# A fused linear-attention and two-MLP kernel on one Trainium2 core: all six moves of a step's output issued by SyncE, with an earlier range column, other stores and a bank of its own

## The chip, the cores and the metric

The kernel runs on one core of a Trainium2 chip (trn2). The metric is the device time of one execution in microseconds (us), as the median over several executions. The core has five engines: TensorE (PE, matmuls; its weight loads are listed as PEld), VectorE (DVE), ScalarE (ACT), GpSimd (POOL) and SyncE (SP, which here only issues DMA transfers). Each engine runs its own instructions in order; they meet through semaphores.

## The reference

Three parts follow one another. The first is a linear attention with a state per batch and head (4 batches, 8 heads, 768 steps, head size 40); the other two are MLPs over 3072 tokens.

```python
# attention, for t in range(S); state is D x D per batch and head
y[:, :, t] = einsum('bhd,bhde->bhe', r_t, state)
Sa    = einsum('bhde,bhe->bhd', state, a_t)
state = state * w_t[:, :, None, :] - einsum('bhd,bhe->bhde', Sa, b_t)
state = state + einsum('bhd,bhe->bhde', v_t, k_t)
# first MLP: d_model 320, d_ff 2048
h = x @ w_in;  x = (h * sigmoid(1.702 * h)) @ w_out
# second MLP: d_ff 1536
g = x @ w_gate;  out = (g * sigmoid(g) * (x @ w_val)) @ w_out2
```

The weights of the MLPs arrive as 64-bit floats and are turned into pairs of 32-bit values (a high and a low part) on the chip; each MLP product is computed from high and low parts (eight matmuls for a product with 320 inputs).

## The kernel before

The attention is cut into 12 steps of 64 time steps. Within a step everything is small matmuls on PE, copies on ACT and masked products on DVE; the state couples one step to the next. Two attention steps make the input of one step of the first MLP (512 tokens), so the first MLP has 6 steps (numbered 0 to 5) of 16 features each (a feature is 128 columns of d_ff). The second MLP also has 6 steps of 512 tokens, with 12 features each.

**The planner.** The attention and the first MLP are not written in a fixed order. Each piece of work is a task with an engine, an estimated cost, what it reads and writes, and a due time (class `Plan`). `order()` simulates the engines with these costs and returns all tasks sorted by their planned begin; where PE would have a gap it adds filler matmuls (`Up.warm`, line 453). Attention tasks have due times by step; those of the MLP are taken when nothing more urgent is ready. The conversion of the first MLP's weights is in this plan too.

**Moves of a step's output.** At the end of an attention step DVE writes the output into `su` (line 1194). `give` (line 1242) then moves it with six DMAs (line 1255) into the tile `xm`, with features on the partitions: three for the first half (`xm0`, issued by SP), three for the second (`xm1`, issued by ACT). ACT and DVE turn `xm` into the high and low parts of the MLP's input `xst` (lines 1262 to 1268).

**First MLP.** `h_part` computes one feature: eight matmuls into the PSUM tile `h` (line 495), Silu on ACT (503), a high part on ACT (509) and a low part `gl` on DVE (510). `o_part`, two features later, adds the product with `w_out` to three PSUM banks, `sums` (lines 522 to 529): `acc[0]` and `acc[1]` with 128 outputs each, and `acc[2]`, whose halves are two partial sums of the last 64 outputs. The weights of two features come from DRAM into one of two buffers `wo` by four DMAs on SP (line 485). After the 16th feature the sums are read out into `sg` buffers: `acc[0]` by DVE (548), `acc[1]` by ACT (545), the upper half of `acc[2]` by ACT (555), and DVE adds the lower half (557). Each result is stored to `x2s` in DRAM by a DMA that ACT issues (551, 559).

**The tail.** When the last attention task has begun (`layer_one`), the rest of the first MLP's tasks, the tail, is run by a loop in `build` (lines 1736 to 1749). After each task marked `last` (the `gl` of a feature) it takes 11 jobs of the conversion of the second MLP's weights (`down.prepare(11)`): loads into `cva` on SP (301), operations on ACT, DVE and POOL, and copies `wg` to `wg` on SP (1387). When 14 PE tasks are left it issues the loads of the second MLP's first input (`load_x(0)`), at 10 it starts to split it, and at 2 it starts the second MLP.

**Second MLP and flag.** `Down.run` does per feature an `h_part` (two groups of eight matmuls, line 1456) and, two features behind, an `o_part` (1475 to 1477). Behind feature 8 of the last step it calls `bad_flag` (line 1295): DVE reduces a column over the smallest weights seen (1299 to 1301), PE transposes it (1303), DVE reduces the row and writes the flag `bad`, by which a branch at the end chooses a slow general version.

Of the kernel before, what the change touches and what calls it, by code (L numbers as in the profile page):

```python
# [386 lines left out]
class Up:  # L387
# [9 lines left out]
    def __init__(self, tc, ctx, keep, cst, w_out, x2s, side):  # L397
# [12 lines left out]
        self.ph = [q.tile([128, 512], F32, name="h")]  # L410
        self.still = k.tile([128, 1], F32R, name="still")
        self.nc.vector.memset(self.still.bitcast(F32), 0.0)  # L412
        self.sums = q.tile([128, 3, 512], F32, name="sums")
        self.acc = [self.sums[:, i] for i in range(3)]
        self.tail = False
        self.hs, self.nsg = 0, 0

    def engine(self, e):
# [38 lines left out]
    def tasks(self, plan):  # L457
# [55 lines left out]
        def o_part(m, i):  # L513
# [24 lines left out]
            if not sp:  # L538
                return
            xs = self.x2s[:, n * m:n * m + n]  # L540
            for k in range(2):
                s = sg_slot()
                t = self.sg[s]
                if k:
                    add("ACT", 0.6, lambda t=t: nc.scalar.activation(out=t, in_=acc[1], func=ACTF.Copy, scale=1 / 1.702),
                        ("acc",), (f"sg{s}",))
                else:
                    add("DVE", 0.7, lambda t=t: nc.vector.tensor_scalar(
                        out=t, in0=acc[0], scalar1=1 / 1.702, scalar2=None, op0=ALU.mult), ("acc",), (f"sg{s}",),
                        port=False)  # L550
                add("ACT", 0.4, lambda t=t, k=k: nc.scalar.dma_start(out=xs[128 * k:128 * k + 128], in_=t),
                    (f"sg{s}",), (), kb=256)
            s = sg_slot()
            t = self.sg[s][0:64]
            add("ACT", 0.6, lambda: nc.scalar.activation(out=t, in_=acc[2][64:128], func=ACTF.Copy, scale=1 / 1.702),
                ("acc",), (f"sg{s}",))
            add("DVE", 0.72, lambda: nc.vector.scalar_tensor_tensor(  # L557
                out=t, in0=acc[2][0:64], scalar=1 / 1.702, in1=t, op0=ALU.mult, op1=ALU.add), ("acc",), (f"sg{s}",), port=False)
            add("ACT", 0.5, lambda: nc.scalar.dma_start(out=xs[256:320], in_=t), (f"sg{s}",), (), kb=128)

        lag = []
        for m in range(B * S // n):
# [10 lines left out]
class Attention:  # L573
# [668 lines left out]
    def give(self, plan, n, due):  # L1242
# [8 lines left out]
            moves.append((t[40 * s:40 * s + 40, 2:4], x[64:104, 2 + s:3 + s].to_broadcast([40, 2, 256]), "xm1"))  # L1251
        moves.append((t[80:120, 2:4], x[64:104, 2:4], "xm1"))
        for i, (o, s, k) in enumerate(moves):
            e, q, cost = ("ACT", nc.scalar, 0.76) if k == "xm1" else ("SP", nc.sync, 0.5)
            plan.add(e, cost, lambda o=o, s=s, q=q: q.dma_start(out=o, in_=s), ("su",), (f"{k}.{i}",), due, kb=80)
        m, half = divmod(n, 2)
        key = f"x{m % 2}.{half}"
# [36 lines left out]

def bad_flag(nc, tc, down, cst, least, good, bad):

    with tc.tile_pool(name="fl2", bufs=1, side="right") as p:
        m = p.tile([128, 1], F32, name="fl_f")
        nc.vector.tensor_reduce(out=m, in_=least, axis=AXL.X, op=ALU.min)
        nc.vector.tensor_scalar(out=m, in0=m, scalar1=TINY, scalar2=None, op0=ALU.is_ge)  # L1300
        nc.vector.tensor_tensor(m, m, good[:, 0:1], op=ALU.mult)
        ps = down.ph.tile([128, 512], F32, tag="gv", name="gv")[0:1, 0:128]
        nc.tensor.transpose(ps, m, cst[:, C_ID:C_ID + 128])
        q = p.tile([1, 1], F32, name="fl_q")
        nc.vector.tensor_reduce(out=q, in_=ps, axis=AXL.X, op=ALU.min)
        nc.vector.tensor_scalar(out=bad, in0=q, scalar1=0.5, scalar2=None, op0=ALU.is_lt)
# [29 lines left out]
class Down:  # L1336
# [168 lines left out]
    def run(self, last):  # L1505
        for m in range(NSTEP):
            parts = iter(())
            for f in range(NF2):
                if m + 1 < NSTEP:
                    if f == 5:  # L1510
                        self.load_x(m + 1)
                    elif f == 8:
                        parts = self.split_x(m + 1)
                if m + f:
                    self.prepare(f=f)
                    self.h_part(m, f)
                    self.lag.append((m, f))
                next(parts, None)
                if m:
                    self.look()  # L1520
                if m == NSTEP - 1 and f == 8:
                    last()
                self.prepare(8)
                if len(self.lag) > self.LAG:
                    self.o_part(*self.lag.pop(0))
                self.prepare(8)
        for x in self.lag:
            self.o_part(*x)
# [171 lines left out]
def build(  # L1700
# [4 lines left out]
    with ExitStack() as ctx:  # L1705
# [5 lines left out]
        with tc.block(schedule_with_timeline_sim=True):  # L1711
# [8 lines left out]
            with conv_ctx, down_ctx, tc.manual_schedule():  # L1720
                conv = Convert(tc, conv_ctx)
                with up_ctx:
# [9 lines left out]
                    first += [words(out1)[q, i] for q in range(4) for i in range(5)]  # L1732
                    down = Down(tc, down_ctx, cst, conv, weights, first, x2s, out, up, least)
                    left = sum(t.eng == "PE" for t in tail)
                    parts = iter(())
                    for t in tail:
                        if t.eng == "PE":
                            if left == 2:
                                down.begin()
                            left -= 1  # L1740
                        t.run()
                        if hasattr(t, "last"):
                            down.prepare(11)
                        if t.eng == "PE":
                            if left == 14:
                                down.load_x(0)
                            elif left == 10:
                                parts = down.split_x(0)
                            next(parts, None)
                down.work(down_ctx)  # L1750
                down.run(lambda: bad_flag(nc, tc, down, cst, least, good, bad))
            rv = nc.values_load(bad, min_val=0, max_val=1)
        with tc.If(rv > 0):
            general(
# [87 lines left out]
```

## Time and profile before

| what | value |
|---|---|
| median of 3 runs | 1118.22 us (1114.80 to 1118.37) |
| the profiled execution's own time | 1112.34 us |
| its span, first to last instruction | 1110.5 us |
| mean granted TensorE clock | 0.985 of full speed |
| PE busy | 1073.1 us (97%), 16682 matmuls |
| DVE / ACT / POOL busy | 702.2 / 436.0 / 98.2 us |

The profile is of one execution. A line number is that of the kernel before. "out<-in" names the tiles written and read. In the timeline a bracket at the end of a row gives the idle time of the engine just before the instruction and what ended it. ACTq and SPq rows are instructions of the queue of that engine that issue DMAs; their time is that of the issue, not of the transfer. Waits are inferred from semaphores, and a wait for several is put down to the last one.

### The profile page before, as it was taken

To read this page: it belongs to the slowest core of one execution; us is meant where nothing else is said; L and a number is where in the kernel's file an instruction comes from. 1 tells how busy PE (TensorE), PEld (TensorE's weight loads), DVE (VectorE), ACT (ScalarE), POOL (GpSimd) and SP (SyncE) were. 2 spreads that over 40 slices of the span, in tenths; PEclk is the share of its full clock that TensorE was granted. 3 is DMA by queue.
4 is the path that set the end of the run, shared out by engine and by line. 5 is a ranking of instruction groups with operands and counts; after the bars stand their busy time and mean duration, and the time that the engine had idled before them with its cause. 6 is when DMAs were issued, how large, how long until landed. Compare 5 with 4: busy or idle time off the path is not lost.

```text
span 1110.5 us, 38519 instructions
## 1 busy us (share of the span) xinstructions
PE 1073.1 (97%) x16682; PEld 892.6 (80%) x16682; DVE 702.2 (63%) x1406; ACT 436.0 (39%) x814; POOL 98.2 (9%) x115
## 2 busy tenths in 40 slices
PE   8999999899999999999999999999999999999987
PEld 7777777678778787888788878888888888888876
DVE  8976797989697887979653667643443343443221
ACT  3443646454343534344343656432222222222221
POOL 0131123320100000000000323210000000000000
PEclk9896999999999999999999999999999999999999
DMA  6265547664353543544224677430423434341000
GB/s 209 73 184 171 180 150 219 180 195 140 113 166 111 161 133 103 162 127 137 87 62 131 201 212 228 142 90 1 141 69 115 124 116 126 96 147 59 24 1 27
DMA packets 141011, 141.88 MB, mean 128 GB/s; under 512 B 16032, under 2 KB 131744, under 8 KB 140832
## 3 DMA queue, kind: packets, MB, share of 16 engines
q1 hardware_dynamic: 134784, 131.48, 39.1%
q10 hardware_dynamic: 6048, 7.86, 2.1%
q8 instruction: 132, 2.16, 0.8%
q14 instruction: 47, 0.39, 0.1%
HBM read 118.04 MB, written 13.11 MB: 118 GB/s over the span
## 4 chain that ended last, share of the span: by engine, by line
PE 87%; DVE 5%; issue 3%; DMA 2%; ACT 1%; SPq 1%; ACTq 0%; POOL 0%; DVEq 0%
PE gv L1456 24%; PE h L495 15%; PE sums L527 4%; PE oacc L1477 4%; PE oacc L1476 4%; PE oacc L1475 4%; PE sums L528 3%; PE sums L529 3%; PE h L453 3%; PE ps L1175 2%; PE sums L523 2%; PE ps L1098 2%; PE sums L522 2%; PE ps L1227 2%; PE ps L740 1%
## 5 line engine op out<-in xcount | busy, mean ns | idle before, releaser
L1456 PE MATMUL gv<-xst,wg 128*128 128x512 f32 x1152 | 279.9, 395 | 0.0
L1456 PEld LDWEIGHTS gv<-xst,wg 128*128 128x128 f32 x1152 | 213.4, 188 | 45.7
L495 PE MATMUL h<-xst,wi 120*128 120x512 f32 x768 | 197.1, 398 | 0.0
L1461 DVE TENSOR_TENSOR sg<-gv,sg 128x512 f32<-128x512 f32 x72 | 49.8, 692 | 186.5 <-PE gv L1456 184.4
L495 PEld LDWEIGHTS h<-xst,wi 120*128 120x128 f32 x768 | 140.5, 188 | 30.6
L503 ACT ACTIVATE sg<-h 128x512 f32<-128x512 f32 x96 | 57.2, 596 | 152.6 <-PE h L495 145.0
L1462 ACT ACTIVATE gh<-sg 128x512 fp32r<-128x512 f32 x72 | 45.5, 632 | 143.0 <-DVE sg L1461 143.0
L510 DVE TENSOR_TENSOR gl<-sg,gh 128x512 fp32r<-128x512 f32 x90 | 63.4, 704 | 60.2 <-ACT gh L509 60.0
L1460 ACT ACTIVATE sg<-gv 128x512 f32<-128x512 f32 x72 | 43.0, 597 | 136.6 <-PE gv L1456 136.6
L323 POOL TENSOR_TENSOR cvw<-cvu,cva 128x256 uint32<-128x256 uint32 (+2 forms) x89 | 71.6, 805 | 274.1 <-DVE cvu L315 168.5
L1476 PE MATMUL oacc<-wo,gh 128*128 128x320 f32 x288 | 89.0, 309 | 0.0
L1477 PE MATMUL oacc<-wo,gl 128*128 128x320 f32 x288 | 89.0, 309 | 0.0
L1475 PE MATMUL oacc<-wo,gh 128*128 128x320 f32 x288 | 89.0, 309 | 0.0
L527 PE MATMUL sums<-gh,wo 128*128 128x512 f32 x192 | 80.8, 421 | 2.9 <-DVE sg L557 2.6
L1463 DVE TENSOR_TENSOR gl<-sg,gh 128x512 fp32r<-128x512 f32 x72 | 49.9, 692 | 50.2 <-ACT gh L1462 50.2
L528 PE MATMUL sums<-gh,wo 128*128 128x512 f32 x192 | 75.5, 393 | 0.0
L529 PE MATMUL sums<-gl,wo 128*128 128x512 f32 x192 | 75.2, 392 | 0.0
L509 ACT ACTIVATE gh<-sg 128x512 fp32r<-128x512 f32 x96 | 60.7, 632 | 3.6 <-ACT sg L503 0.3
L788 DVE TENSOR_TENSOR tsol<-tsol,tmp 128x126 f32<-128x126 f32 (+22 forms) x217 | 56.3, 260 | 6.7
L780 DVE TENSOR_TENSOR tmp<-tsol,nsol 128x126 f32<-128x126 f32 (+22 forms) x217 | 55.8, 257 | 6.9
L453 PE MATMUL h<-still 128*128 128x512 f32 x183 | 58.3, 466 | 1.1 <-DVE still L412 1.1
L1476 PEld LDWEIGHTS oacc<-wo,gh 128*128 128x128 f32 x288 | 54.1, 188 | 3.2
(182 smaller groups left out, 1618.8 us busy)
## 6 DMA issues: line engine op xcount, KB each, us to landing
wo<-w_out SPq DMA_DIRECT2D x192, 160.0 KB
cva<-out SPq DMA_DIRECT2D x128, 128.0 KB
cva<-gv SPq DMA_DIRECT2D x96, 128.0 KB
kb<-kba SPq DMA_DIRECT2D x92, 104.0 KB
cva<-in_ab SPq DMA_DIRECT2D x64, 120.0 KB
r<-rT SPq DMA_DIRECT2D x48, 104.0 KB
vt<-vT SPq DMA_DIRECT2D x48, 104.0 KB
a<-kba SPq DMA_DIRECT2D x46, 104.0 KB
```

Of the source, the lines that this page charges most:

```text
L323: nc.gpsimd.tensor_tensor(w.bitcast(U32), u, lo, op=ALU.add)
L453: self.nc.tensor.matmul(self.ph[0], c.to_broadcast([128, 128]), c.to_broadcast([128, 512]), start=True, stop=True)
L495: nc.tensor.matmul(ps[:, 0:n], self.wi[:, b, 128 * f:128 * f + 128], x[:, a], start=(e == 0), stop=(e == 7))
L509: add("ACT", 0.63, lambda: nc.scalar.activation(out=hi, in_=sg, func=ACTF.Copy), (f"sg{s}",), (f"gh{d}",))
L510: add(("DVE", "POOL"), (0.74, 1.35), lambda e: self.engine(e).tensor_tensor(lo, sg, hi.bitcast(F32), op=ALU.subtract), (f"sg{s}", f"gh{d}" ...
L527: nc.tensor.matmul(acc[k], w[:, c:c + 128], hi, start=st, stop=False)
L528: nc.tensor.matmul(acc[k], w[:, 256 + c:384 + c], hi, start=False, stop=False)
L529: nc.tensor.matmul(acc[k], w[:, c:c + 128], lo, start=False, stop=sp)
L1456: nc.tensor.matmul(ps, w[:, b], x[:, a], start=(i == 0), stop=(i == 7))
L1475: nc.tensor.matmul(acc[k], hi[:, c], self.wo[:, f, 0], start=st, stop=False)
L1476: nc.tensor.matmul(acc[k], hi[:, c], self.wo[:, f, 1], start=False, stop=False)
L1477: nc.tensor.matmul(acc[k], lo[:, c], self.wo[:, f, 0], start=False, stop=sp)
```

## The change

- `give`: all six moves are issued by SP, with a planned cost of 0.6 each (before 0.5 on SP and 0.76 on ACT).
- Readout of the sums: ACT reads `acc[0]` and `acc[1]`, DVE both halves of `acc[2]`; the three stores are issued after all of these; `acc[2]` becomes a tile of its own (`third`) in place of the third bank of `sums`. In the tail SP issues the stores.
- Tail: the SP tasks (loads of `wo`) are put off until behind the next task marked `last`, and behind that task's conversion jobs; no conversion jobs are taken between two such tasks if a task of the readout lies between them; `load_x(0)` comes at 20 PE tasks left in place of 14.
- `bad_flag` becomes a generator: its column (DVE) is made behind feature 7 of the last step, the transpose and the rest behind feature 10.

```diff
@@ Up.__init__
-        self.sums = q.tile([128, 3, 512], F32, name="sums")
-        self.acc = [self.sums[:, i] for i in range(3)]
-        self.tail = False
+        self.sums = q.tile([128, 2, 512], F32, name="sums")
+        self.acc = [self.sums[:, 0], self.sums[:, 1], q.tile([128, 512], F32, name="third")]
+        self.tail, self.stores = False, tc.nc.scalar
@@ Up.tasks, o_part
+            first = len(plan.tasks)
+            moves = []
             for k in range(2):
                 s = sg_slot()
                 t = self.sg[s]
-                if k:
-                    add("ACT", 0.6, lambda t=t: nc.scalar.activation(out=t, in_=acc[1], func=ACTF.Copy, scale=1 / 1.702),
-                        ("acc",), (f"sg{s}",))
-                else:
-                    add("DVE", 0.7, lambda t=t: nc.vector.tensor_scalar(
-                        out=t, in0=acc[0], scalar1=1 / 1.702, scalar2=None, op0=ALU.mult), ("acc",), (f"sg{s}",),
-                        port=False)
-                add("ACT", 0.4, lambda t=t, k=k: nc.scalar.dma_start(out=xs[128 * k:128 * k + 128], in_=t),
-                    (f"sg{s}",), (), kb=256)
+                add("ACT", 0.6, lambda t=t, k=k: nc.scalar.activation(out=t, in_=acc[k], func=ACTF.Copy, scale=1 / 1.702),
+                    ("acc",), (f"sg{s}",))
+                moves.append((xs[128 * k:128 * k + 128], t, s, 256))
             s = sg_slot()
             t = self.sg[s][0:64]
-            add("ACT", 0.6, lambda: nc.scalar.activation(out=t, in_=acc[2][64:128], func=ACTF.Copy, scale=1 / 1.702),
-                ("acc",), (f"sg{s}",))
+            add("DVE", 0.65, lambda: nc.vector.tensor_scalar(
+                out=t, in0=acc[2][64:128], scalar1=1 / 1.702, scalar2=None, op0=ALU.mult), ("acc",), (f"sg{s}",),
+                port=False)
             add("DVE", 0.72, lambda: nc.vector.scalar_tensor_tensor(
                 out=t, in0=acc[2][0:64], scalar=1 / 1.702, in1=t, op0=ALU.mult, op1=ALU.add), ("acc",), (f"sg{s}",), port=False)
-            add("ACT", 0.5, lambda: nc.scalar.dma_start(out=xs[256:320], in_=t), (f"sg{s}",), (), kb=128)
+            moves.append((xs[256:320], t, s, 128))
+            for o, t, s, kb in moves:
+                add("ACT", 0.4, lambda o=o, t=t: self.stores.dma_start(out=o, in_=t), (f"sg{s}",), (), kb=kb)
+            for t0 in plan.tasks[first:]:
+                t0.out = True
@@ Attention.give
-            e, q, cost = ("ACT", nc.scalar, 0.76) if k == "xm1" else ("SP", nc.sync, 0.5)
+            e, q, cost = "SP", nc.sync, 0.6
@@ bad_flag
         nc.vector.tensor_tensor(m, m, good[:, 0:1], op=ALU.mult)
+        yield
         ps = down.ph.tile([128, 512], F32, tag="gv", name="gv")[0:1, 0:128]
@@ Down.run
-                if m == NSTEP - 1 and f == 8:
-                    last()
+                if m == NSTEP - 1 and f in (7, 10):
+                    next(last, None)
@@ build
-                    parts = iter(())
-                    for t in tail:
+                    parts, later, up.stores = iter(()), [], nc.sync
+                    for i, t in enumerate(tail):
+                        if t.eng == "SP":
+                            later.append(t)
+                            continue
...
                         if hasattr(t, "last"):
-                            down.prepare(11)
+                            ends = [hasattr(x, "last") for x in tail[i + 1:]] + [True]
+                            if not any(hasattr(x, "out") for x in tail[i + 1:i + 1 + ends.index(True)]):
+                                down.prepare(11)
+                            for x in later:
+                                x.run()
+                            later = []
                         if t.eng == "PE":
-                            if left == 14:
+                            if left == 20:
                                 down.load_x(0)
...
+                    for x in later:
+                        x.run()
                 down.work(down_ctx)
-                down.run(lambda: bad_flag(nc, tc, down, cst, least, good, bad))
+                down.run(bad_flag(nc, tc, down, cst, least, good, bad))
```

## Rows read from the trace of the kernel before

**Rows 1.** Stages: stretch, its length, busy time of each engine (instructions), clock, DMA.
```profile
70.00:125.00 55.00, 49.20 (x1479) 38.78 (x1481) 41.63 (x71) 24.73 (x53) 8.72 (x12) 0.81 0.55 169
...
642.00:654.00 12.00, 9.44 (x42) 7.39 (x41) 7.96 (x17) 7.88 (x17) 2.30 (x3) 1.00 0.72 217
...
718.00:1078.00 360.00, 360.00 (x1838) 312.40 (x1837) 142.64 (x268) 97.14 (x171) 4.48 (x6) 1.00 0.28 86
```

**Rows 2.** Waits of PE: what waited, for what; total us, times, longest.
```profile
PE gv L1303 <- DVE fl_f L1301: 2.9, 1, 2.9
PE sums L527 <- DVE sg L557: 2.6, 1, 2.6
...
PE ps L1012 <- ACT md L647: 1.7, 1, 1.7
PE ps L995 <- ACT tok L647: 1.6, 2, 1.1
```

**Rows 3.** Timeline around the flag: start us, us, engine, line, operation.
```profile
1074.95 3.89 PE L1456 MATMUL gv<-xst,wg 128*128 128x512 f32 x16
...
1080.33 0.69 DVE L1463 TENSOR_TENSOR gl<-sg,gh 128x512 fp32r<-128x512 f32 x1 [0.70 <-ACT gh L1462]
...
1083.58 3.89 PE L1456 MATMUL gv<-xst,wg 128*128 128x512 f32 x16
...
1089.07 3.89 PE L1456 MATMUL gv<-xst,wg 128*128 128x512 f32 x16
```

**Rows 4.** Timeline of ACT where step 4's sums are read out.
```profile
648.60 0.44 ACT L307 ACTIVATE cva<-cva 128x256 uint32<-128x256 uint32 x1 [1.29 <-DMA cva<-gv]
...
649.25 0.58 ACT L545 ACTIVATE sg<-sums 128x512 f32<-128x512 f32 x1
```

**Rows 5.** Timeline of ACT where step 5's sums are read out.
```profile
709.29 0.60 ACT L545 ACTIVATE sg<-sums 128x512 f32<-128x512 f32 x1 [2.21 <-PE sums L522]
...
710.65 0.59 ACT L555 ACTIVATE sg<-sums 64x512 f32<-64x512 f32 x1 [0.76 <-DVE sg L548]
```

**Rows 6.** Timeline of DVE in the same stretch.
```profile
709.92 0.69 DVE L548 TENSOR_SCALAR sg<-sums 128x512 f32<-128x512 f32 x1 [2.12 <-ACT sg L545]
711.27 0.68 DVE L557 SCALAR_TENSOR_TENSOR sg<-sums,sg 64x512 f32<-64x512 f32 x1 [0.66 <-ACT sg L555]
```

**Rows 7.** Tile xm: its moves, ns min/median/max; who waited (us, times).
```profile
L1255 ACTq DMA_DIRECT2D xm<-su x36: 772/809/1383, 66.9 to 595.9; - x36
L1255 SPq DMA_DIRECT2D xm<-su x36: 706/716/1422, 67.9 to 595.1; - x36
...
  ACT md L647: 9.4, 2
  ACT tok L647: 5.2, 2
```

**Rows 8.** Timeline of ACT at the fourth step's moves.
```profile
220.32 0.70 ACT L647 ACTIVATE md<-ps 104x640 f32<-104x640 f32 x1 [5.64 <-DMA xm<-su]
```

**Rows 9.** Timeline of SP (its DMA issues) at the second step's moves.
```profile
112.03 2.33 SPq L1255 DMA_DIRECT2D xm<-su  x3
```

**Rows 10.** Timeline of ACT in the same stretch.
```profile
118.42 1.32 ACT L1262 ACTIVATE xst<-xm 120x256 fp32r<-120x256 f32 x4
```

**Rows 11.** Timeline of PE in the same stretch.
```profile
125.51 2.11 PE L495 MATMUL h<-xst,wi 120*128 120x512 f32 x8
```

**Rows 12.** Filler matmuls of line 453 alone: stretch, length, busy time.
```profile
70.00:125.00 55.00, 18.30 (x48) 10.63 (x46) 0.81 0.55 169
```

**Rows 13.** SP's DMA issues in the first layer's tail.
```profile
635.85 1.80 SPq L485 DMA_DIRECT2D wo<-w_out  x4
...
640.29 2.73 SPq L1387 DMA_DIRECT2D wg<-wg  x4
643.11 1.98 SPq L485 DMA_DIRECT2D wo<-w_out  x4
```

**Rows 14.** The chain that ended last, in time: start us, us, what.
```profile
645.62 2.89 DMA cva<-gv
```

More of the change, by code (lines that the diff above doesn't have):

```diff
@@ L1295, in bad_flag @@
 def bad_flag(nc, tc, down, cst, least, good, bad):
+    assert not down.looks and not down.seen
     with tc.tile_pool(name="fl2", bufs=1, side="right") as p:
```

## Prediction, made before the result was known

> **What bounds the kernel now.** I read the table of stages first [rows 1]. From 718 to 1078 us TensorE (PE) is busy for all 360 us, so nothing that other engines gain there moves the end: time can only come from places where PE stands still, or where it runs work that is not needed. The reader should look for three of them. In 70 to 125 us PE is busy 49.20 of 55 us, but 18.30 us of this are filler matmuls of line 453 [rows 12], and the granted clock is 0.81 of the full 2.4 GHz, a mixture of both levels. There the end is set by the chain through DVE, ACT, DMA and PE of the attention steps, until the first group of the MLP starts at 125.51 us [rows 11]. In 642 to 654 us PE is busy 9.44 of 12 us. The third place needs the list of PE's waits [rows 2]: the flag's transpose waits 2.9 us for VectorE.
>
> Then I read the timeline around each of these, and the tile xm, which is what the six moves write [rows 7]. They cost 0.716 us each on SP and 0.809 us each on ACT, 36 on either, three and three in each of 12 steps. ACT is an in-order engine: the copies behind the three moves wait until su is ready and the moves are issued (9.4 us before md, 5.2 us before tok) [rows 7]. In the fourth step ACT stood still for 5.64 us before md [rows 8]. PE then waited 1.7 us for md, and in two other steps 1.6 us for tok [rows 2].
>
> **The change, part by part.**
>
> *The flag in two parts (line 1295).* From one feature's first matmuls to the next it takes 1083.58 - 1074.95 = 8.63 us across the flag and 1089.07 - 1083.58 = 5.49 us in the next one [rows 3]: 3.1 us lost. The three VectorE operations on the flag's column stand in program order behind the gl of feature 8, which starts only at 1080.33 [rows 3], after PE had finished that feature's matmuls, and the transpose stands in PE's queue in front of the next group. With the column reduced at feature 7 and the transpose issued at feature 10, its input is some 2 x 5.49 = 11 us old. What is left is the transpose itself. Bounds 2.8 to 3.1; I take 3.0. The result is there 11 us later, but feature 11 (5.49 us) and three more groups of output matmuls still follow, so nothing at the end waits for it.
>
> *Reading out the sums.* After the last group of step 5, ACT and VectorE had nothing else to do, and still the four reads ran one behind the other: ACT 709.29, DVE 709.92, ACT 710.65, DVE 711.27 [rows 5, 6], 2.66 us in all; they wait for one another although they read three banks, since all three banks are one tile. With the third bank a tile of its own, ACT reads banks 0 and 1 (2 x 0.60 = 1.2 us) beside VectorE's two operations on the third (0.68 + 0.69 = 1.4 us). At the end of step 4, ACT came to its first read only at 649.25, behind conversion work that itself waited 1.29 us for a load [rows 4], and PE's next group waited 2.6 us for the last read, the only such wait of the run [rows 2]. The change also leaves out the 11 conversion jobs ahead of such a readout. 1.4 us fit under the one group of h matmuls (7.26 us for four groups, below, so 1.8) that PE runs in between. Bounds: 0, if something else holds ACT or VectorE, to 2.6; I take 2.5. At the other five ends PE doesn't wait, so they give nothing. The jobs left out, three or four times 11, go to the next stage, where VectorE is busy 142.64 and ACT 97.14 of 360 us [rows 1]: cost nothing; if that cover were gone they would cost up to 44 x 0.69 = 30 us, the duration of a VectorE operation in [rows 3].
>
> *The moves on SP.* ACT loses 36 x 0.809 = 29.1 us of issue and its stalls behind su. PE gets back at most the 1.7 + 1.6 = 3.3 us of waits behind md and tok, and nothing if the rearranged order makes others of them. I take 2.3, nearer the top, because the blocking itself is gone. SP gets 36 x 0.716 = 25.8 us more, 2.15 us per step, behind the first three moves that wait for the same su already; queued behind are the loads of the next step, which have most of a step's time where PE is full of MLP work. Not so in the first two steps: xm1 is complete six issues after su (4.3 us) where it was three of ACT's (2.4 us), 1.9 us later. In step 1 SP starts at 112.03 [rows 9], so the last issue ends near 116.4, and with 2.89 us for a landing (a load of the tail [rows 14]) the data are there at 119.3; ACT read xm from 118.42 for 1.32 us [rows 10], and the first h group came at 125.51 [rows 11]. Measured slack is thus there, but the order comes from the planner, whose costs go from 3 x 0.76 = 2.28 to 6 x 0.6 = 3.6, 1.3 us more before the first h group. Each us there is paid in full, since PE only runs fillers meanwhile. Bounds 0 to 1.9 lost; I take 0.9.
>
> The Trainium skill, page "DMA: Bandwidth & Descriptors", section "Issuing engines are not separate DMA queues", says that issuing from several engines saves the sequencer's issue time and no more. This speaks against the change, which gives up exactly that saving; by the rule alone the first two steps would lose the full 1.9 us, and the sum below would be 5.9 in place of 6.9. The trace agrees that both engines issue side by side.
>
> *Tail, rest.* The stores of the sums by SP and the earlier load of x have no reader for many features: nothing. The weight loads wo, however, are put behind the next block of conversion jobs on SP; see the third rival.
>
> Sum: 3.0 + 2.5 + 2.3 - 0.9 = 6.9 us faster. The profiled execution took 1112.34 us, giving 1105.4. The median of the runs, 1118.22, is 1.0053 times as long as the profiled one, so I forecast 1111.3 us, a ratio of 0.9938.
>
> **The rivals.**
>
> *The startup gives it back.* The planner orders the whole first part anew, because several costs differ. Fillers (18.30 us) and a granted clock of 0.81 in 70 to 125 us [rows 1, 12] show that this stretch depends on order: PE work outside the fillers is 30.9 us, and some of it ran at the lower level. If the first h group comes 5 us later, the gain falls to 1.9 us: 1116.3, no change. Against it: the slack of 5 us between the conversion of xm and that group.
>
> *The opposite, a shorter startup.* With ACT free of 2.4 us of issue per step the first h group could come 4 us sooner: 1107. Nothing in the rows shows ACT as what that group waited for.
>
> *Late weights, slower.* Two wo loads are 7.26 us apart, one for four groups [rows 13]; a load may start when its buffer's last reader ends, five groups before its first reader, 9.1 us. Issue and landing take 1.80 + 2.89 = 4.7 us [rows 13, 14], so 4.4 us are spare. Behind a further block of jobs, the load of 635.85 would go out after the conversions' loads, 2 to 4 us later; but if the copies wg to wg are in that block (2.73 us, from 640.29 [rows 13]), it goes out at 643.0, 7.2 us later, and PE waits 2.8 us. It decides above 4.4 us. Between the two readouts, 649.25 and 709.29 [rows 4, 5], lie 60.0 / 7.26 = 8 loads; if each makes PE wait 2 us, 16 us are lost, 9.1 more than gained: 1127 us. Above 10.3 / 8 = 1.3 us each the kernel is slower by 0.3%. Against it: only one piece in seven or eight has such copies.
>
> *It does not do what it says.* ACT or VectorE is still late at step 4's end, or PE still waits for the flag; one term of 2.5 to 3.0 stays, and the gain is 4.1: 1114.1.
>
> **How the numbers follow.** Forecast 0.60 (1108 to 1115); startup gives it back 0.15; shorter startup 0.07; late weights 0.10; doesn't do it 0.08. A difference below 0.3%, 3.4 us, can hardly be told from no change. Faster by more: 0.57 of the first case, 0.07, and half of the last, 0.04, sum 0.68. Slower: 0.10 and 0.02 of the startup case. Same: the remaining 0.20. The range from 1105 to 1119 leaves out late weights, a startup that costs more than 7 us, and a shorter startup that saves more than 6 us: under 2 in 10.
>
> **What would show it.** Right: the features 7 to 11 of the last step are all 5.5 to 5.8 us apart; after step 4's last group PE goes on without a wait for sg; ACT has no wait for xm; two chains of reads end some 1.4 us after the last group. Startup: the first h group (line 495) between 124 and 128 us, with 16 to 21 us of fillers in the 55 us before it. Wrong: that group after 130, waits of the sums' matmuls for wo in the tail, or new waits of PE for kb, a or wdec, whose loads now stand behind six moves.

## The result and the profile after

The changed kernel takes 1131.22 us (median of 6 runs, 1129.73 to 1139.29), the kernel before 1116.80 us (6 runs, 1113.99 to 1118.37): a ratio of 1.0144 (95% interval 1.0120 to 1.0168). It is slower by about 14 us; the forecast was 1111.3 us, in a range from 1105 to 1119, with 0.12 for slower.

The profiled execution of the changed kernel has a span of 1127.9 us. Busy times and clock in three stages, cut at the first group of the first MLP and at the first group of the second (stretch, its length, busy time of PE, PEld, DVE, ACT, POOL, granted clock, DMA share, GB/s), for the changed kernel:

```profile
0.00:121.60 121.60, 104.44 (x3085) 85.20 (x3085) 100.43 (x165) 51.87 (x104) 24.07 (x34) 0.97 0.54 163
121.60:722.80 601.20, 574.91 (x11571) 464.56 (x11569) 443.34 (x939) 275.04 (x517) 76.96 (x77) 0.98 0.48 146
722.80:1127.90 405.10, 398.99 (x2034) 346.17 (x2032) 158.60 (x299) 108.87 (x194) 6.74 (x9) 1.00 0.28 85
```

The same view of the kernel before:

```profile
0.00:125.50 125.50, 113.40 (x3084) 91.35 (x3084) 101.44 (x166) 49.83 (x102) 21.00 (x32) 0.88 0.52 157
125.50:701.70 576.20, 560.55 (x11568) 455.48 (x11566) 442.40 (x943) 277.37 (x519) 70.48 (x75) 1.00 0.51 153
701.70:1110.50 408.80, 399.15 (x2034) 345.81 (x2032) 158.40 (x299) 108.81 (x194) 6.71 (x9) 1.00 0.27 83
```

The first stage is 3.9 us shorter and the last 3.7 us. The loss is in the middle one, 25.0 us: PE runs the same matmuls (some 11570), but stands still for 601.20 - 574.91 = 26.29 us where it was 15.65, and is busy 14.4 us longer at a lower mean clock. That makes 17.4 us between these two executions; the medians differ by 14.4 us. The waits of PE that answer to [rows 2] (what waited, for what; total us, times, longest):

```profile
PE third L522 <- DVE sg L554: 4.1, 1, 4.1
...
PE sums L527 <- DMA wo<-w_out: 2.3, 2, 1.6
...
PE ps L1037 <- DVE sv L1234: 2.0, 2, 1.5
...
PE sums L529 <- DVE gl L510: 1.3, 1, 1.3
```

The waits for fl_f and md are gone, as forecast. Among the new ones are these four, three of them for DVE. The timeline shows the largest, where the sums of the first MLP's third step are read out (start us, us, engine, line, operation; in brackets the idle time before and what ended it):

```profile
468.11 4.41 POOL L715 TENSOR_TENSOR kb<-kb,rc 104x1024 f32<-104x1024 f32 x2 [8.96 <-DMA vt<-vT]
468.27 2.17 DVE L781 TENSOR_TENSOR tmp<-tsol,nsol 128x115 f32<-128x115 f32 x1
470.47 2.18 DVE L789 TENSOR_TENSOR tsol<-tsol,tmp 128x115 f32<-128x115 f32 x1
...
480.75 6.64 ACTq L558 DMA_DIRECT2D x2s<-sg  x3
...
484.77 0.68 DVE L510 TENSOR_TENSOR gl<-sg,gh 128x512 fp32r<-128x512 f32 x1
485.49 0.69 DVE L551 TENSOR_SCALAR sg<-third 64x512 f32<-64x512 f32 x1
486.22 0.68 DVE L554 SCALAR_TENSOR_TENSOR sg<-third,sg 64x512 f32<-64x512 f32 x1
...
486.95 0.50 PE L522 MATMUL third<-gh,wo 128*128 128x512 f32 x1 [4.11 <-DVE sg L554]
...
487.43 0.60 ACT L503 ACTIVATE sg<-h 128x512 f32<-128x512 f32 x1 [6.22 <-DVE sg L554]
```

The bank was complete at 480.3 (its last matmul starts at 479.92 and takes 0.39 us). VectorE's two reads stood in its queue behind a chain of 47 small operations of the attention, run since 464.06 (lines 781 and 789, 0.2 to 0.3 us each but for the two shown), and began at 485.49. PE waited 4.11 us for them, and ACT, whose stores stand behind the same reads, 6.22 us. Ten microseconds of PE at a time, here and behind it:

```profile
480.00:490.00 10.00, 5.89 (x125) 4.25 (x126) 9.38 (x27) 2.32 (x4) 0.00 (x0) 0.89 0.32 99
490.00:500.00 10.00, 9.88 (x252) 7.69 (x239) 8.73 (x22) 4.60 (x7) 0.00 (x0) 0.76 0.22 64
500.00:510.00 10.00, 10.00 (x221) 8.15 (x221) 9.04 (x32) 5.26 (x9) 0.00 (x0) 1.00 0.37 111
```

PE stands still, and behind it the granted clock is 0.76 for 10 us of full work: a mixture of 1.2 and 2.4 GHz. Here a stall is followed by low clock; whether it must be isn't shown. Two longer stretches hold all the clock that the changed kernel lacks in this stage. The changed kernel:

```profile
130.00:250.00 120.00, 109.55 (x2942) 86.98 (x2935) 91.00 (x161) 63.91 (x132) 33.81 (x31) 0.94 0.58 179
440.00:620.00 180.00, 170.59 (x3605) 138.46 (x3604) 122.92 (x273) 67.19 (x114) 12.62 (x7) 0.96 0.35 106
```

The kernel before:

```profile
130.00:250.00 120.00, 111.76 (x3200) 88.64 (x3203) 100.32 (x185) 66.46 (x137) 32.85 (x31) 1.00 0.63 190
440.00:620.00 180.00, 178.10 (x3484) 146.00 (x3483) 129.38 (x299) 74.10 (x131) 5.45 (x7) 1.00 0.39 119
```

An estimate of what the clock took is busy time multiplied by what the clock lacks to 1, added up over pieces of 10 us: 5.8 us in the first stretch and 6.4 us in the second. The first can't be laid on the change: there PE is idle nearly as long in both (10.4 and 8.2 us), and kernels with the order of before lost between 0.0 and 7.5 us of clock there (e2 and e12, below). The second can: no kernel without the loss has any low clock there. In it PE is idle 7.5 us longer (9.4 against 1.9), which with the 6.4 us makes 13.9 between these two executions, about the 14 us of the medians.

The issues of a step's moves show something larger (timeline of SP's queue, changed kernel, two steps in a row):

```profile
454.55 1.55 SPq L1256 DMA_DIRECT2D xm<-su  x2
...
529.80 1.55 SPq L1256 DMA_DIRECT2D xm<-su  x2
```

The same two steps in the kernel before:

```profile
450.49 0.77 SPq L1255 DMA_DIRECT2D xm<-su  x1
...
500.41 0.76 SPq L1255 DMA_DIRECT2D xm<-su  x1
```

Before, the attention keeps a beat of 50 us for a step here. After the change one step takes 75.25 us; later steps make up some of it, and the last one's moves begin at 609.76 us where they began at 593.51.

### The profile page after: what moved, and what is told of

It is laid out like the page before. It is cut to its first block, busy times and chain, and to the rows that moved or that the text cites. A ratio compares the mean times of both kernels' runs of the same rounds, so it can differ in the third digit from the quotient of the medians.

```text
span 1127.9 us, 38533 instructions
## 1 busy us (share of the span) xinstructions
PE 1078.3 (96%) x16685; PEld 895.9 (79%) x16685; DVE 702.4 (62%) x1401; ACT 435.8 (39%) x814; POOL 107.8 (10%) x120
## 3 DMA queue, kind: packets, MB, share of 16 engines
q8 instruction: 133, 2.18, 0.8%
## 4 chain that ended last, share of the span: by engine, by line
PE 82%; DVE 7%; issue 4%; DMA 4%; ACT 1%; SPq 1%; ACTq 0%; POOL 0%; DVEq 0%
PE gv L1459 24%; PE h L495 13%; PE sums L527 4%; PE oacc L1480 4%; PE oacc L1479 4%; PE oacc L1478 4%; PE sums L528 3%; PE sums L529 3%; PE ps L1176 2%; PE h L453 2%; PE ps L1099 2%; PE third L523 2%; PE ps L1228 2%; PE third L522 2%; PE ps L741 1%
## 5 line engine op out<-in xcount | busy, mean ns | idle before, releaser
L495 PE MATMUL h<-xst,wi 120*128 120x512 f32 x768 | 202.2, 406 | 0.0
L495 PEld LDWEIGHTS h<-xst,wi 120*128 120x128 f32 x768 | 143.6, 192 | 31.4 <-issue 0.2
L323 POOL TENSOR_TENSOR cvw<-cvu,cva 128x256 uint32<-128x256 uint32 (+2 forms) x89 | 77.1, 866 | 354.4 <-DVE cvu L310 116.3
L527 PE MATMUL sums<-gh,wo 128*128 128x512 f32 x192 | 81.8, 426 | 2.9 <-DMA wo<-w_out 2.3
L1466 DVE TENSOR_TENSOR gl<-sg,gh 128x512 fp32r<-128x512 f32 x72 | 49.9, 692 | 50.2 <-ACT gh L1465 50.2
L528 PE MATMUL sums<-gh,wo 128*128 128x512 f32 x192 | 77.2, 402 | 0.4 <-DMA wo<-w_out 0.3
L1478 PEld LDWEIGHTS oacc<-wo,gh 128*128 128x128 f32 x288 | 54.1, 188 | 3.2 <-issue 0.2
L1479 PEld LDWEIGHTS oacc<-wo,gh 128*128 128x128 f32 x288 | 54.1, 188 | 3.2
```

The costliest lines, as they stand in the source:

```text
L323: nc.gpsimd.tensor_tensor(w.bitcast(U32), u, lo, op=ALU.add)
L495: nc.tensor.matmul(ps[:, 0:n], self.wi[:, b, 128 * f:128 * f + 128], x[:, a], start=(e == 0), stop=(e == 7))
L527: nc.tensor.matmul(acc[k], w[:, c:c + 128], hi, start=st, stop=False)
L528: nc.tensor.matmul(acc[k], w[:, 256 + c:384 + c], hi, start=False, stop=False)
L1478: nc.tensor.matmul(acc[k], hi[:, c], self.wo[:, f, 0], start=st, stop=False)
L1479: nc.tensor.matmul(acc[k], hi[:, c], self.wo[:, f, 1], start=False, stop=False)
```

## The experiments

Four questions, 18 kernels. Each ratio is to runs of the kernel before on the same chip; the medians of before differ from chip to chip (1115 to 1123 us), so ratios are compared here, not times.

**Is it the moves on SP, or the order that the planner deals out?** The moves alone, in a new order; the moves on SP in the old order; the change with the old moves; the changed order with three moves back on ACT. The edits are all in `give`:

```diff
 e1 (from before):  e, q, cost = "SP", nc.sync, 0.6
 e2 (from before):  e, q, cost = ("ACT", nc.sync, 0.76) if k == "xm1" else ("SP", nc.sync, 0.5)
 e3 (from after):   e, q, cost = ("ACT", nc.scalar, 0.76) if k == "xm1" else ("SP", nc.sync, 0.5)
 e4 (from after):   e, q, cost = "SP", nc.scalar if k == "xm1" else nc.sync, 0.6
```

> The kernel before with one part of the change: all six moves of a step are planned and issued on SyncE at 0.6 each (readout, tail and flag as before). Order theory (the loss comes from the order in which the planner deals the tasks out, which any new cost makes anew): a new order, so some time between 1112 and 1132 us, and whatever it loses against 1116.8 stands in the trace between the first and the second MLP as waits of TensorE with a granted clock below 1.00 behind them. Queue theory (six moves on SyncE delay what SyncE loads next, whatever the order): 1127 to 1133 us. Readout theory (the two reads of the third bank by VectorE are late behind the attention's small operations): 1114 to 1118 us, since this kernel has the readout of before.

> The kernel before, planned as before (three moves counted as ScalarE's at 0.76), but all six are issued by SyncE. TensorE, VectorE and GpSimd keep every instruction in the order of before. Order theory: 1114 to 1119 us, and TensorE's stretch between the first and second MLP within 3 us of the 576.2 us of before. Queue theory: 1127 to 1133 us, with waits of TensorE for the loads of x or for weights behind SyncE's moves. Readout theory: 1114 to 1118 us as well.

> The changed kernel with the moves put back as before (three on ScalarE at 0.76, three on SyncE at 0.5, planned so); readout, tail and flag as changed. Order theory: again a new order, a time between 1108 and 1131 us, with the loss wherever TensorE has gaps with a low clock behind them between the first and the second MLP. Queue theory: 1109 to 1115 us (the change without its costly part). Readout theory: 1127 to 1132 us, with TensorE again waiting about 4 us for VectorE's second read of the third bank.

> The changed kernel, planned as changed (six moves counted as SyncE's at 0.6), but the three moves of the second kind are issued by ScalarE. TensorE, VectorE and GpSimd keep every instruction in the order of the changed kernel. Order theory: 1128 to 1134 us, the stretch between the first and second MLP within 4 us of the 601.2 us of the changed kernel. Queue theory: 1112 to 1118 us. Readout theory: 1127 to 1133 us, the 4 us wait at the third bank included.

Measured: e1 1134.34 us, 1.0165 (1.0133 to 1.0196); e2 1116.55, 1.0006 (0.9974 to 1.0037); e3 1113.96, 0.9984 (0.9956 to 1.0012); e4 1131.13, 1.0130 (1.0095 to 1.0166). The middle stage of e2, by engine as above:

```profile
122.10:701.30 579.20, 561.80 (x11567) 456.34 (x11566) 441.46 (x942) 277.60 (x519) 69.81 (x75) 1.00 0.50 152
```

The same stage of e4:

```profile
122.20:717.90 595.70, 571.14 (x11570) 460.49 (x11569) 443.18 (x939) 275.02 (x517) 77.30 (x77) 0.99 0.48 147
```

The queue theory falls from both sides: six moves issued by SP cost nothing that can be told in the old order, and taking three off SP gives nothing back that can be told in the new one. What carries the loss is the order. In e1 a different order with the old readout loses as much, so the new readout isn't needed for it. There too the largest wait of PE between 440 and 600 us is for VectorE's last read of the sums:

```profile
PE sums L527 <- DVE sg L557: 6.3, 2, 5.3
```

Not all came as expected: e1 lies 2 us above the range of the order theory, and e4's stage of 595.7 us lies 1.5 us outside the 4 us that I had allowed around 601.2. The time of e3 fits both theories; e2 and e4 are what separates them.

**Is the stall at 487 us the loss?** Three 104x1024 products of one attention step had been planned on POOL. e5 gives them to DVE, at the same place; e9 also moves the two reads of `third` forward in DVE's queue; e6 does the reverse of e5 to the kernel before.

```diff
-  plan.add(("DVE", "POOL"), (1.25, 2.2), scale_a, (ck,), (ak,), due + 0.13)
+  plan.add(("DVE", "POOL"), (1.25, 2.2), lambda e: scale_a("DVE" if n == 10 else e), (ck,), (ak,), due + 0.13)
   # e5, e9: the same for scale(1, e) and scale(0, e); e6: "POOL", in the kernel before
     order = plan.order()
+    for t in [t for t in order if hasattr(t, "out") and t.eng == "DVE"][4:6]:    # e9 alone
+        order.remove(t)
+        order.insert(1 + max(order.index(d) for d in t.deps), t)
```

> The changed kernel with every instruction of TensorE in the order of the changed kernel; only the three 104x1024 products of one attention step (a at 456.96 us, kb twice from 468.11 us), which the planner gave to GpSimd, are issued by VectorE in their place. If these three are what holds VectorE's chain up and so makes TensorE wait 4.1 us at the third bank at 486.95 us (and lose clock behind it): the wait shrinks below 1 us, and 1131.2 us falls by 5 to 9 us, to 1122 to 1126 us. If that stall is only one of several of the new order, the other part (some 10 us before 300 us and after 500 us) stays. If VectorE is late by its own load and not by GpSimd: no gain, 1129 to 1134 us, the wait of 4 us still there.

> The kernel before, TensorE's order as before; the three 104x1024 products of the same attention step, which VectorE computes there, are issued by GpSimd. If such products on GpSimd beside VectorE's chain cost what the changed kernel lost there: a new wait of TensorE of 2 to 5 us near 460 to 500 us, a granted clock below 1.00 behind it, and 1120 to 1124 us. If they only cost where the order already lets TensorE run dry: 1114 to 1118 us.

> The changed kernel, TensorE's order kept; the three 104x1024 products of that step on VectorE as in e5_scales_on_dve, and VectorE's two reads of the third bank at the end of that step moved ahead to right behind the sums in the program (six small operations earlier in VectorE's queue). The 2.3 us that e5_scales_on_dve still waited there should fall below 0.5 us. If this stall and the clock behind it are a separable part of the loss: 4 to 7 us less than the changed kernel, 1124 to 1127 us where it takes 1131. If the time comes back as stalls elsewhere (TensorE only reaches the next late result sooner): no gain over e5_scales_on_dve.

Measured: e5 1133.78 us, 1.0103 (1.0069 to 1.0137); e6 1119.36, 0.9980 (0.9948 to 1.0013); e9 1129.29, 1.0106 (1.0059 to 1.0153). In e5 the wait at the bank is 2.3 us in place of 4.1, and not below 1 us as expected; one of the three products, 1.21 us at 484.74, now stands between VectorE's two reads. In e9 the wait is gone, but some microseconds later PE waits for another result of DVE (timeline of PE in e9):

```profile
492.63 1.45 PE L741 MATMUL ps<-kb,a 40*32 40x32 f32 x128 [2.18 <-DVE nk L999]
```

By the mid values about a quarter of the loss goes with this stall (1.0144 and 1.0130 become 1.0103 and 1.0106, with intervals that overlap). It is one symptom of the order, not the cause, and POOL's products cost nothing in the order of before.

**Are plans with six moves on SP bad, or was this one a bad deal?** Only the number or engine in `give` is altered: e7 plans ACT's three at 0.70 in place of 0.76; e8, f4 and f5 are e1 with 0.5, 0.65 and 0.8; f6 is the whole changed kernel with 0.5.

> The kernel before, the same instructions on the same engines; only the number that the planner is given for one of ScalarE's three moves is 0.70 in place of 0.76, which deals out a new order. If any new order loses what the changed one lost (the old order being a lucky one): 1125 to 1135 us. If orders scatter: somewhere between 1110 and 1132 us. If it is the planned engine of the moves and not the order as such: 1113 to 1119 us.

> The kernel before with all six moves planned on and issued by SyncE, at the 0.5 each that its three were planned at before, in place of 0.6. If planning six moves on SyncE is what makes the order a bad one: 1127 to 1135 us as with 0.6 each. If the value 0.6 happened to deal a bad order: any time between 1110 and 1132 us, and less than 1125 us would show that the engine alone isn't the reason.

> The kernel before with all six moves planned on and issued by SyncE at 0.65 each (0.5 gave 1.0005, 0.6 gave 1.0165). If a plan with six moves of some 0.6 on SyncE systematically deals a bad order (each step's x that much later in the plan): 1.010 to 1.020 again. If 0.6 was one bad deal among orders that scatter: within 0.5% of before as likely as not.

> The same with 0.80 each, about what six moves took on SyncE in the traces (4.8 us for six). If a plan nearer to the measured times deals a better order: 0.995 to 1.003. If the lateness of x in the plan is what costs: worse than at 0.6, 1.015 to 1.030. If orders scatter: anything from 0.997 to 1.020.

> The whole changed kernel with one number altered: the six moves planned at 0.5 each on SyncE in place of 0.6. If the number 0.6 dealt the bad order: 0.995 to 1.003. If six moves planned on SyncE together with the changed readout deal bad orders: 1.010 or more, with TensorE's waits for VectorE at the end of a step before 600 us.

Measured: e7 1.0000 (0.9966 to 1.0035); e8 1.0005 (0.9974 to 1.0035); f4 1.0041 (1.0014 to 1.0068); f5 1.0017 (0.9991 to 1.0043); f6 1124.87 us, 1.0018 (0.9987 to 1.0049). Every one of these is a new order, and none has the loss; only f4 is slower than before by more than its interval, by 0.4%. The whole change, with one planning number at 0.5 in place of 0.6, is level with the kernel before. f6 in the middle stage:

```profile
126.80:712.60 585.80, 565.00 (x11565) 455.63 (x11565) 438.02 (x932) 274.82 (x513) 72.36 (x76) 1.00 0.50 150
```

The moves of the same two steps in f6:

```profile
455.64 0.78 SPq L1256 DMA_DIRECT2D xm<-su  x1
...
505.56 0.79 SPq L1256 DMA_DIRECT2D xm<-su  x1
```

**What are the other parts worth?** e10 is the kernel before with the flag in two halves; g2 is e10 again on another chip; e12 is e10 with `third` a tile of its own. All three keep the order of before. e11 is e3 with the tail's loads of `wo` in place and its stores on ACT. f3 is the whole change, but with the engines and costs of before told to the planner, and so the old order; g1 is f3 with e11's tail.

```diff
 f3, in o_part (and in give as e2):
-    add("ACT", 0.6, lambda t=t, k=k: nc.scalar.activation(out=t, in_=acc[k], func=ACTF.Copy, scale=1 / 1.702),
-        ("acc",), (f"sg{s}",))
+    read = lambda t=t, k=k: nc.scalar.activation(out=t, in_=acc[k], func=ACTF.Copy, scale=1 / 1.702)
+    if k: add("ACT", 0.6, read, ("acc",), (f"sg{s}",))
+    else: add("DVE", 0.7, read, ("acc",), (f"sg{s}",), port=False)
...
 e11 and g1, in build:
-    parts, later, up.stores = iter(()), [], nc.sync
+    parts = iter(())
...
-    if t.eng == "SP":
-        later.append(t)
-        continue
...
-    for x in later:
-        x.run()
```

> The kernel before with one part of the change, the flag computed in two halves, 7 and 10 features into the last step; nothing that the planner sees is touched, so the order stays. By the forecast's sum: the wait of 2.9 us for fl_f is gone and the time falls by 2.8 to 3.1 us (ratio 0.997 to 0.998). Rival: the second half waits for something else there, no gain.

> e10_flag_alone a second time, on the same chip as g1_old_order_old_tail: 0.993 to 0.998 if its first ratio of 0.9946 holds; nearer to 0.9974 (2.9 us) if the first one was helped by scatter.

> The kernel before, its order kept, with the flag in two halves and the third bank a tile of its own (readout, moves and tail as before). Expected: the 2.9 us of the flag, and at the end of the fifth step 0.5 to 1.5 us of the 2.6 us wait for VectorE's read, since the next sums' first matmuls no longer wait for the third bank: ratio 0.996 to 0.997. Rival: the readout gives nothing, the same as e10_flag_alone.

> The changed kernel with the moves of before (as e3_after_old_moves) and, after the attention's end, loads of wo in their place and stores of sums on ScalarE again; third tile, readout and flag as changed. If e3_after_old_moves lost its 4.3 us of waits for wo by the loads being pushed behind the step's end: these waits are gone, and the time is 4 to 6 us below e3_after_old_moves, a ratio to before of 0.993 to 0.995. If ScalarE's stores then hold its next sg up: new waits of TensorE for sg of 1 to 3 us at the ends of steps, and no gain.

> The whole change (six moves by SyncE, readout by ScalarE, ScalarE, VectorE twice, third tile, stores and loads after the attention's end and the flag as changed), with the planner given the engines and costs of before, so that TensorE keeps the order of before but for the flag's one matmul. Order theory: the 14 us are gone: -3 for the flag, -1 to -2.5 at the end of the fifth step, +2 to +4 for late weights wo, a time of 1111 to 1117 us and a ratio of 0.995 to 1.000. If the new instructions themselves were the loss, in whatever order: 1.010 or more.

> As f3_all_old_order, but after the attention's end the loads of wo stand in their place again and the stores of sums are ScalarE's. If the late weights ate what flag and readout gave in f3_all_old_order: no wait of TensorE for wo after 600 us, and a ratio of 0.994 to 0.998. If the moves on SyncE or the new readout cost as much as the flag gives: 0.999 to 1.003.

Measured: e10 1112.22 us, 0.9946 (0.9922 to 0.9969); g2 1119.34, 0.9971 (0.9945 to 0.9997); e12 1110.79, 0.9952 (0.9926 to 0.9979); e11 1114.60, 0.9976 (0.9951 to 1.0002); f3 1124.44, 1.0009 (0.9977 to 1.0041); g1 1124.50, 1.0020 (0.9997 to 1.0044). The waits of PE in e12 from 640 us to the end of the first MLP:

```profile
PE sums L527 <- DVE sg L548: 1.4, 1, 1.4
```

Those in g1, from 600 us:

```profile
PE h L495 <- ACT sg L503: 3.6, 2, 2.8
```

Those in f3, from 600 us:

```profile
PE sums L527 <- DMA wo<-w_out: 2.7, 3, 1.5
PE sums L528 <- DMA wo<-w_out: 0.5, 1, 0.5
```

The flag alone gives 0.3% in g2, as forecast, and 0.5% in e10, more than forecast. f3 lies just above its range and far from the 1.010 of its rival: with the old order the loss is gone. The 2.6 us wait at step 4's end [rows 2] doesn't vanish, it changes its name: 2.7 + 0.5 = 3.2 us for late weights in f3, and 3.6 us for ACT's Silu in g1, whose ACT carries two reads and three stores. e11 shows the same wait, 3.0 us, and no gain over e3: the second case of its expectation. Only in e12, with the tile of its own and the old readout, is it shorter, 1.4 us; the time of e12 can't be told from that of e10. g1 came out as the second case of its expectation too: without late weights it is no faster than f3, and by the mid values the rest of the change costs about as much as the flag gives. Which part of it does wasn't separated.

**All kernels by one view each.** PE's idle time is length minus busy time of the middle stage; waits are PE's listed waits from 440 to 600 us; the beat is from the moves of SP near 455 us to the next step's.

| kernel | ratio | PE idle, us | waits 440 to 600, us | beat, us |
|---|---|---|---|---|
| before | 1 | 15.7 | 1.1 | 49.9 |
| e2, moves on SP, old order | 1.0006 | 17.4 | 0 | 49.9 |
| e6, products on POOL, old order | 0.9980 | 18.3 | 1.1 | 49.9 |
| e10, g2, flag, old order | 0.9946, 0.9971 | 19.3, 17.8 | 1.6, 1.5 | 50.1, 49.3 |
| e12, flag and third, old order | 0.9952 | 16.5 | 1.6 | 50.0 |
| f3, g1, whole change, old order | 1.0009, 1.0020 | 20.6, 19.5 | 0.6, 0.2 | 49.9, 49.9 |
| e3, e11, old moves | 0.9984, 0.9976 | 19.2, 19.1 | 1.3, 0.8 | 50.2, 50.1 |
| f6, whole change at 0.5 | 1.0018 | 20.8 | 0.9 | 49.9 |
| e7, e8 | 1.0000, 1.0005 | 17.7, 18.0 | 1.9, 1.1 | 51.2, 50.0 |
| f5, f4 | 1.0017, 1.0041 | 20.1, 21.5 | 2.7, 1.0 | 53.1, 48.4 |
| **after** | 1.0144 | 26.3 | 8.4 | 75.3 |
| e4, order of after | 1.0130 | 24.6 | 7.4 | 75.4 |
| e5, e9, order of after | 1.0103, 1.0106 | 26.0, 25.4 | 6.1, 6.2 | 71.9, 71.4 |
| e1, moves alone at 0.6 | 1.0165 | 30.7 | 10.0 | 69.1 |

Five kernels are more than 1% slower, and they are the five whose beat is broken near 455 us, with 6 to 10 us of waits behind it. No kernel of the other fifteen has either. The clock says the same: between 440 and 620 us it is 1.00 in every 10 us of all fifteen, while by the estimate above the five lose 2.7 to 6.4 us there. A late attention alone doesn't cost: in e7 the last moves begin at 616.75 us, later than in the changed kernel, at 1.0000.

## Why the prediction was wrong

**The flag held.** I took 3.0. In the last step the groups of matmuls of features 8 to 11 follow one another without a hole (after, timeline of PE, to compare with [rows 3]):

```profile
1096.04 3.89 PE L1459 MATMUL gv<-xst,wg 128*128 128x512 f32 x16
...
1101.52 3.89 PE L1459 MATMUL gv<-xst,wg 128*128 128x512 f32 x16
...
1107.01 3.89 PE L1459 MATMUL gv<-xst,wg 128*128 128x512 f32 x16
...
1110.74 0.27 PE L1306 MATMUL gv<-cst,fl_f 128*1 128x128 f32 x1
...
1112.61 3.90 PE L1459 MATMUL gv<-xst,wg 128*128 128x512 f32 x16
```

They are 5.48, 5.49 and, across the transpose, 5.60 us apart, where it was 8.63 across the flag. The transpose at 1110.74 waits for nothing; e10 and g2 give the price.

**The startup can't be told.** I took 0.9 us lost there. The group came at 121.59, before the 124 to 128 of the rival, after 17.10 us of fillers in the 55 us before it. But the kernel before had it at 125.51, and e10 and g2, which have the same startup instruction for instruction, had it at 119.27 and 123.69: executions alone differ by 6 us there, so neither a gain of 3.9 us nor a loss of 0.9 is shown. The same holds for the 1.9 us that the prediction worked out by the rule of the Trainium skill, page "DMA: Bandwidth & Descriptors", section "Issuing engines are not separate DMA queues": no run here shows it. e2, with the same moves and the old order, is at 1.0006 as a whole, and 1.9 us would be 0.0017, inside its interval. Six issues take 4.86 us on SP where I assumed 4.3: the two broadcast moves take 0.79 to 0.81 us each there as well, and small gaps lie between the issues.

**The moves term failed, and it is the step that decides.** "PE gets back at most the 1.7 + 1.6 = 3.3 us of waits behind md and tok, and nothing if the rearranged order makes others of them": the lower bound of 0 was the mistake. An order dealt anew can make more waits than it removes; this one made 7.3 us of them between 440 and 600 us (8.4 against 1.1), and low clock in the same stretch. The rival that spoke of a new order put it into the startup alone ("the planner orders the whole first part anew ... this stretch depends on order"), because my table of stages [rows 1] has 70 to 125, 642 to 654 and 718 to 1078 us, and nothing of the 517 us between the first two. They were left out as PE was full there; but that it is full is a property of the order, which the change dealt out again. The size of the term itself was small: e2 has the moves without a new order, and 1.0006. ACT's waits for xm didn't vanish as I expected either: those before md and tok are gone, but those before the copies into xst grew from 5.0 us (6 times) to 11.3 us (10 times).

**The readout term failed as well.** "At the other five ends PE doesn't wait, so they give nothing": at the third step's end PE waited 4.1 us in this order for two reads on DVE behind the attention's chain. At step 4's end the 2.5 us were not had: the readout itself was side by side as forecast (ACT 666.85 to 667.93, DVE 667.26 to 668.66), but 0.65 us for ACT's Silu and 2.6 us for late wo came instead (the rival "late weights", at its mechanism, at 2.6 us in place of 16). f3 shows late weights in the old order as well. The conversion jobs left out cost nothing, as I took it, but not by going to the last stage: its counts of DVE and ACT instructions, 299 and 194, are those of before.

So the sum, term by term in the runs: flag 3 to 6 us gained (e10, g2); the moves nothing that can be told (e2); the startup open; moves, readout and tail together 4 to 8 us lost, where I had 2.3 + 2.5 = 4.8 gained (f3 and g1 against e10 and g2); the new order some 14 to 15 lost, where I had nothing (the changed kernel against f3, g1 and f6, which have the whole change without this order).

The chip's part in the stall was the pair of small VectorE operations at 468.27 and 470.47, 2.17 and 2.18 us where their neighbours take 0.27, for just the 4.41 us of two GpSimd products. In e5, where VectorE does the products itself, the same two take 0.28 us each. The Trainium skill, page "SBUF — State Buffer", section "SBUF: two separate sides", says that a VectorE operation with two inputs in SBUF and a GpSimd operation that reads SBUF lock each other out for a whole instruction; the trace agrees. e5 shows what moving the products gives here: 1.8 us less wait at the bank, and no difference in the time that can be told.

**What stays open.** Why the planner's deal breaks the beat at 0.6 and not at 0.5, 0.65 or 0.8 wasn't traced through the planner. That the stalls bring the low clock isn't shown: no run filled a stall to see the clock return, and in e2 PE was idle for 9.7 us between 130 and 250 us with the clock at 1.00 throughout. And f3 and g1 lack 0.4 to 0.7% against e10 and g2, of which PE's waits in the tail (3.2 and 3.6 us against 2.7) explain only a little. Both slow orders come from plans with six moves at 0.6.

**A version that beats both.** The flag in two halves, in the order of before, with or without the third tile: 0.9946 to 0.9971, some 19 to 22 us below the changed kernel by the ratios.

## What to carry to other kernels

Where a planner orders the work, a changed cost or engine is two changes: the instruction, and a new order of everything. Price them apart (issue the new instruction under the old plan, and the old instruction under the new plan) before believing either; one number, 0.5 or 0.6, decided here between no loss and 1.4%. And put every stage that the planner touches into the forecast, the full ones too: here all was lost in one that I had left out because PE was full there.

## What the runs showed that was not expected

- Orders of nearly the same work differ by up to 1.8% (0.9984 to 1.0165), with eight new orders tried: six within 0.5% of the old one, two 1.3 to 1.7% slower. With the moves alone changed, the planned cost decided between 1.0005 (0.5) and 1.0165 (0.6).
- The loss came in two parts of like size. Between 440 and 620 us the changed kernel idles 7.5 us more and by the estimate above lost 6.4 us of clock, at 0.69 to 0.97 in four pieces of 10 us.
- The clock of one execution says little by itself before 250 us. The kernel before shows 1.00 there and e12, with its order, this:

```profile
140.00:150.00 10.00, 9.12 (x145) 7.73 (x144) 6.28 (x13) 1.96 (x4) 0.74 (x1) 0.51 0.20 52
```

- A move of the broadcast kind takes 0.79 to 0.81 us of issue on SP (at 456.97 in the changed kernel) and 0.80 to 0.81 on ACT (at 450.46 in the kernel before); [rows 7] looked as if the engine set the price.
